# A fused attention and feed-forward backward kernel: dV up to eight heads ahead of dK, and the columns of dq as a stream of four a head

## The chip, the cores and the metric

The kernel runs on one core of a Trainium2 chip. The metric is device microseconds (us) of one execution. The kernel before takes 1714.82 us, the median of three runs (1712.49 to 1715.11); the execution whose profile is read below took 1712.58 us, and its trace spans 1710.6 us.

The profile calls the engines PE (TensorE; PEld are its weight loads), DVE (VectorE), ACT (ScalarE), POOL (GpSimd) and SP (SyncE). In this kernel SP computes nothing. It issues nearly all large DMAs, one after another in program order. An issue that has to wait for something holds up every issue behind it.

## What is computed

A decode step of a transformer block with one new token for each of 4 sequences, and its whole backward pass. Cut to what matters:

```python
# B=4 sequences, H=32 heads, Sk=4096 cached keys, Dh=128, D=512, F=1792, all bf16
q = layernorm(x) @ wq                                  # (4, 32, 1, 128)
p = softmax(einsum("bhqd,bhkd->bhqk", q, k_cache) * Dh ** -0.5)
o = einsum("bhqk,bhkd->bhqd", p, v_cache)
h = x + o @ wo
out = h + (silu(ln(h) @ w1) * (ln(h) @ w3)) @ w2
# outputs: out and the gradients of x, k_cache, v_cache, wq, wo, w1, w3, w2
```

There are 4 * 32 = 128 pairs of sequence and head, called heads here. Each has 1 MB of K and 1 MB of V. For one head, with the row dO of 128 numbers, P of 4096 numbers and the number c = sum(dO * O):

```python
dV = outer(P, dO)                  # 4096 x 128: needs P and dO, not V
dP = V @ dO                        # needs V read a second time, and transposed
dS = P * (dP - c) * scale
dK = outer(dS, q)                  # 4096 x 128
dq = scale * (M @ dO - c * kP)     # M is a 128x128 matrix, kept from the forward part
```

So the forward part reads K and V (256 MB), and the backward part reads V again (128 MB) and writes dV and dK (256 MB).

## The kernel before

SBUF is cut into 23 slots of 1 MB each. A tile of K, V, dK or dV takes a slot from a queue of free ones and gives it back. The next user of the slot waits, by semaphore, until the last one is done with it, and for a written gradient that means until its DMA has landed. During the forward part 8 slots fill up with the matrices M, 16 heads to a slot; they are free only when the columns of dq have been computed from them.

The functions of the backward part that the change and the prediction touch:

```python
def outer(dst, col2, row):                      # one DVE multiply of 128x4096
    nc.vector.tensor_tensor(out=..., in0=col2..., in1=row..., op=ALU.mult)

def grad_V(s):
    gv = Slot("gv")
    outer(gv.heads(), P2s.pop(s), reps["rdo", s // REP][:, s % REP, :])
    nc.sync.dma_start(out=rows_of(out_3[b, h]), in_=gv.heads())
    ...                                          # gives the slot back (0 and 1: later)

def front(s):                                    # dP of head s
    hl = s % B
    for g in range(SJ // GW):                    # 4 groups of 8 transposes on PE,
        V_T(s, psT, range(g, g + 1))             # each copied back by ACT
    ...
    dO_window(s + 2)                             # POOL
    ...  # 8 matmuls into rows["acc"]; after four heads one group of dP is complete
    # the slot of V goes to the ring of the V loads, or to the free ones

def group_dS(g): ...                             # DVE: dS of four heads at once

def grad_K(s):
    gk = Slot("gk")
    outer(gk.heads(), dS2s[s // B][:, s % B], reps["rq", s // REP][:, s % REP, :])
    nc.sync.dma_start(out=rows_of(out_2[b, h]), in_=gk.heads())
    gk.give()

def P_pairs(s): ...                              # POOL: P of a head in pairs, 3 buffers
def load_V2(eng): ...                            # SP: the second load of V
```

The side work is a generator that is advanced by some steps a head. It begins with the columns of dq:

```python
def side_work():
    ...
    for s in range(NH):
        nc.tensor.matmul(dq_ps[:, s:s + 1], lhsT=M_of(s)[:, 0:Dh], rhs=dOT_f[:, s:s + 1], start=True, stop=True)
        if s % MC == MC - 1:
            Ms[s // MC].give()
            ...                                  # loads wq again into a freed slot
        if s % 3 == 2:
            yield
    ...                                          # then dq, dx, and the gradients of the weights
```

A second generator, `rest_of_dO` (unit "o"), computes dO for the heads from 32 on; it runs from head 2, one step a head. The main loop:

```python
O0, S0, L, LV = 2, 21, 5, 3
for s in range(L):                               # lead-in
    load_ahead(s); P_pairs(s); front(s)
    if s < 2:
        first_gv[s].give()                       # slots of dV 0 and 1
    elif s < LV + 1:
        grad_V(s)                                # dV of heads 2 and 3
group_dS(0)
for s in range(NH):
    load_ahead(s + L)
    if s % REP == 0 and s + REP < NH:
        replicate(s + REP)                       # rows of dO and of q on all partitions
    P_pairs(s + L)
    if s + L < NH:
        front(s + L)
    ...
    if s > 0 and s + LV < NH:
        grad_V(s + LV)                           # dV three heads ahead
    grad_K(s)
    if s % B == B - 1 and s + 1 < NH:
        group_dS((s + 1) // B)
    if s >= S0:
        step("s", 3 if s < S0 + 15 else 2)
    elif s >= O0:
        step("o")
```

Of the kernel before, what the change touches and what calls it, by code (L numbers as in the profile page):

```python
# [9 lines left out]
FP32 = mybir.dt.float32  # L10
# [14 lines left out]
def kernel(  # L25
# [22 lines left out]
    nc = tc.nc  # L48
    P = nc.NUM_PARTITIONS
# [5 lines left out]
    Dh = A_k_cache.shape[3]  # L55
    F = B_w1.shape[1]
    NH = B * H
    HD = H * Dh
    assert NH == P and Dh == P and H == 32 and Sk == 32 * P
    assert D == 4 * P and F % P == 0  # L60
    DC = D // P
# [5 lines left out]
    MC = 16  # L67
# [3 lines left out]
    x2 = A_x.rearrange("b s d -> (b s) d")  # L71
# [12 lines left out]
    def bh_of(s):  # L84
        return s % B, s // B

    def rows_of(ap):
        return ap.rearrange("(p j) d -> p j d", p=P)
# [74 lines left out]
    ident_b = const.tile([P, P], BF16, name="ident_b")  # L163
# [14 lines left out]
    def ones_window(col):  # L178
# [11 lines left out]
                          in_=rowg[:, None, :, None].to_broadcast([P, 4, 8, 4]))  # L190
# [70 lines left out]
    with ExitStack() as c0:  # L261
# [11 lines left out]
        for h in range(H):  # L273
            for cc in range(DC):
                nc.tensor.matmul(qT_ps[:, h, :], lhsT=wq_s[cc].b(HD)[:, h * Dh:(h + 1) * Dh], rhs=xhatT[:, cc, :],
                                 start=(cc == 0), stop=(cc == DC - 1))
# [4 lines left out]
        for r in range(2):  # L281
            for t_ in range(2):
                for q in range(4):
                    nc.tensor.matmul(qr_ps[32 * q:32 * (q + 1), 2 * r + t_, :], lhsT=ident_b[:, 64 * r + t_:64 * (r + 1):2],
                                     rhs=qT_bf[:], start=True, stop=True, tile_position=(0, 32 * q))
# [3 lines left out]
    Ms = []  # L289

    def M_of(s):
        return Ms[s // MC].f(MC * (Dh + 1)).rearrange("p (n c) -> p n c", c=Dh + 1)[:, s % MC, :]
# [214 lines left out]
    def d_hh_units():  # L507
        w2 = load_w2()
        w2T = two_slots("w2T")
        gT = fw.tile([P, DC, B], BF16, name="gT", tag="gT", bufs=1)  # L510
        yield
        yield
        pt = psX.tile([P, DC, B], FP32, tag="x", name="pt_gT")
        for c in range(DC):
            nc.tensor.transpose(pt[:, c, :], gr[0:B, c * P:(c + 1) * P], ident_f[0:B, 0:B])
        nc.vector.tensor_copy(out=gT[:], in_=pt[:])
        nc.vector.tensor_copy(out=grT[:], in_=pt[:])
        gr_s.give()
        yield
        for jj in range(DC):  # L520
            for i in range(2):
                pt = psT.tile([P, GW, P], BF16, tag="tps", name="pt_w2")
                for k in range(7):
                    nc.tensor.transpose(pt[:, k, :], w2_view(w2, 7 * i + k)[:, jj * P:(jj + 1) * P], ident_b[:])
                nc.scalar.copy(out=w13_view(w2T, jj).rearrange("q (p c) -> q p c", c=FC)[:, :, i * 7:(i + 1) * 7],
                               in_=pt[:, 0:7, :].rearrange("q c p -> q p c"))
                yield
        for sl in w2:
            sl.give()
        ps = psX.tile([P, FC, B], FP32, tag="x", name="dhh_ps")  # L530
        for fc in range(FC):
            for jj in range(DC):
                nc.tensor.matmul(ps[:, fc, :], lhsT=w13_view(w2T, jj)[:, fc * P:(fc + 1) * P], rhs=gT[:, jj, :],
                                 start=(jj == 0), stop=(jj == DC - 1))
        nc.vector.tensor_copy(out=d_hhT[:], in_=ps[:])
        for sl in w2T:
            sl.give()
# [60 lines left out]
    units = {"d": d_hh_units()}  # L598

    def step(k, n=1):  # L600
        for _ in range(n):
            next(units[k], None)
# [113 lines left out]
    dOT_f = pers2.tile([P, NH], FP32, name="dOT_f")  # L716
    dOrows_bf = pers2.tile([NH, Dh], BF16, name="dOrows_bf")
# [4 lines left out]
    qrows_bf = pers2.tile([NH, Dh], BF16, name="qrows_bf")  # L722
# [29 lines left out]
    REP = B  # L752
    reps = {}
# [13 lines left out]
    P2s, first_gv = {}, []  # L767
# [9 lines left out]
    def grad_V(s):  # L777
        b, h = bh_of(s)
# [3 lines that stand above are left out]
        if s > 1:  # L782
            gv.give()
        else:
            first_gv.append(gv)
# [14 lines left out]
    with ExitStack() as cm:  # L800
# [33 lines left out]
        for wi, wt in enumerate((w1, w3)):  # L834
            for fc in range(FC):
                for cc in range(DC):
                    nc.tensor.matmul(gu_ps[:, wi, fc, :], lhsT=w13_view(wt, cc)[:, fc * P:(fc + 1) * P], rhs=hhatT[:, cc, :],
                                     start=(cc == 0), stop=(cc == DC - 1))
# [25 lines left out]
        for jj in range(DC):  # L864
            i_mm = 0
            for (lt, wt) in ((d_gateT_bf, w1), (d_upT_bf, w3)):
                for fc in range(FC):
                    nc.tensor.matmul(dn_ps[:, jj, :], lhsT=w13_view(wt, jj)[:, fc * P:(fc + 1) * P], rhs=lt[:, fc, :],
                                     start=(i_mm == 0), stop=(i_mm == 2 * FC - 1))
                    i_mm += 1  # L870
        for sl in w1 + w3:
            sl.give()
        rs = Slot("reps")
        rep_bufs = {nm_: [rs.b()[:, (2 * k + i) * 512:(2 * k + i + 1) * 512].rearrange("p (i d) -> p i d", i=REP) for i in range(2)]
                    for k, nm_ in enumerate(("rq", "rdo"))}
# [4 lines left out]
        ps = psA.tile([P, REP, Dh], FP32, tag="rT", name="repq_ps")  # L880
# [4 lines left out]
        for s in range(3):  # L885
# [8 lines left out]
                         start=True, stop=True)  # L894
# [14 lines left out]
        for b0, b1 in ((0, 1), (1, B)):  # L909
            ps = psA.tile([P, B, Dh], FP32, tag="rT", name="rep_ps")  # L910
            for b in range(b0, b1):
                for jj in range(DC):
                    nc.tensor.matmul(ps[:, b, :], lhsT=dhT[:, jj, b:b + 1].to_broadcast([P, P]), rhs=wo_page(0)[:, 0, jj, :],
                                     start=(jj == 0), stop=(jj == DC - 1))
# [12 lines left out]
    with ExitStack() as c2:  # L927
        psT = c2.enter_context(tc.tile_pool(name="psT2", bufs=2, space=bass.MemoryType.PSUM))
        psD = c2.enter_context(tc.tile_pool(name="psD", bufs=1, space=bass.MemoryType.PSUM))
        psrep = c2.enter_context(tc.tile_pool(name="psrep", bufs=1, space=bass.MemoryType.PSUM))  # L930
        psg = c2.enter_context(tc.tile_pool(name="psg", bufs=2, space=bass.MemoryType.PSUM))
        psx = c2.enter_context(tc.tile_pool(name="psx", bufs=1, space=bass.MemoryType.PSUM))
# [15 lines left out]
            gu.append((dst, ps, n))  # L948


        def side_work():
            pt = psg.tile([P, Dh], BF16, tag="gps", name="pt_O")
            nc.tensor.transpose(pt[:], OT_bf[:], ident_b[:])
            nc.scalar.copy(out=O_sb[:], in_=pt[:])
            dq_ps = psx.tile([P, 512], FP32, tag="x2", name="dq_ps")
            wq2s = deque()

            def load_wq2(cc):
                if cc < DC:
                    wq2s.append(Slot("wq2"))  # L960
                    nc.sync.dma_start(out=wq2s[-1].b(HD), in_=A_wq[cc * P:(cc + 1) * P, :])

            for s in range(NH):
                nc.tensor.matmul(dq_ps[:, s:s + 1], lhsT=M_of(s)[:, 0:Dh], rhs=dOT_f[:, s:s + 1], start=True, stop=True)
                if s % MC == MC - 1:
                    Ms[s // MC].give()
                    if s // MC in (3, 5):
                        load_wq2(s // MC // 2 - 1)
                if s % 3 == 2:
                    yield  # L970
            yield
            t = rs.f(2080)[:, 1536:1536 + NH]
            nc.vector.tensor_tensor(out=t, in0=c_rep[:], in1=kPT[:], op=ALU.mult)
# [13 lines left out]
            for cc in range(DC):  # L987
                wq2 = wq2s.popleft()
# [8 lines left out]
                for h in range(H):  # L997
                    nc.tensor.matmul(dx_ps[0:B, cc * P:(cc + 1) * P], lhsT=dqT_bf[:, h * B:(h + 1) * B], rhs=wv[:, h, :],
                                     start=(h == 0), stop=(h == H - 1))
# [62 lines left out]
            for i in range(2):  # L1062
                st = Slot("gw2")
                hw = hh_rows[:, i * 7 * P:(i + 1) * 7 * P].rearrange("b (p k) -> b k p", k=7)
                for k in range(7):
# [4 lines left out]
                                  in_=st.b(7 * D).rearrange("p (c j) -> p c j", c=7))  # L1070
# [4 lines left out]
            for (rows, out_ap) in ((dg_rows, out_6), (du_rows, out_7)):  # L1075
                for i in range(2):
                    st = Slot("gw13")
                    nw = hhat_bf[0:B, i * 2 * P:(i + 1) * 2 * P].rearrange("b (p k) -> b k p", k=2)
                    for k in range(2):
                        for (f0_, w_) in f_chunks:  # L1080
# [5 lines left out]
                                      in_=st.b(2 * F).rearrange("p (c f) -> p c f", c=2))  # L1086
                    st.give()
            r1.give()
            for h0 in range(0, H, 8):
                st = Slot("gwo")  # L1090
                ow = oflat.b(HD)[0:B, h0 * P:(h0 + 8) * P].rearrange("b (p k) -> b k p", k=8)
                for k in range(8):
# [4 lines left out]
                                  in_=st.b(8 * D).rearrange("p (k j) -> p k j", k=8))  # L1097
                st.give()
            oflat.give()
            r2.give()  # L1100

        units["s"] = side_work()


# [13 lines left out]
            nc.scalar.copy(out=dh, in_=dr_ps[:])  # L1118

        units["o"] = rest_of_dO()  # L1120
        def replicate(i0):
            K_ = 8 * B if i0 < 8 * B else P
            for nm_, rows in (("rdo", dOrows_bf), ("rq", qrows_bf)):
                if (nm_, i0 // REP) in reps:
                    continue
                ps = psrep.tile([P, REP, Dh], FP32, tag="rep", name="rep_ps")
                for i in range(REP):
                    nc.tensor.matmul(ps[:, i, :], lhsT=ident_b[0:K_, i0 + i:i0 + i + 1].to_broadcast([K_, P]), rhs=rows[0:K_, :],
                                     start=True, stop=True)
                rt = rep_bufs[nm_][i0 // REP % 2]  # L1130
                nc.scalar.copy(out=rt, in_=ps[:])  # L1131
                reps[nm_, i0 // REP] = rt

        rows = {}
        dS2s = {}
# [4 lines left out]
        def dO_window(s):  # L1140
            if s < NH:
                nc.gpsimd.tensor_copy(out=zd[s % B][:, 32:132:67], in_=dOT_bf[:, s:s + 1].to_broadcast([P, 2]))  # L1142

        def P_pairs(s):
            if s < NH and s not in P2s:
                P2s[s] = bw3.tile([P, SJ, 2], BF16, tag="P2", name="P2")
                nc.gpsimd.tensor_copy(out=P2s[s][:], in_=P_all[:, s, :, None].to_broadcast([P, SJ, 2]))  # L1147
# [58 lines left out]
                load_V2(nc.sync)  # L1206


        O0, S0, L, LV = 2, 21, 5, 3

        def load_ahead(s):
            prefetch()
# [2 lines left out]

        for s in range(2):
            dO_window(s)
        for s in range(L):
            load_ahead(s)
            P_pairs(s)  # L1220
            front(s)
            if s < 2:
                first_gv[s].give()
            elif s < LV + 1:
                grad_V(s)
        group_dS(0)
        for s in range(NH):
            load_ahead(s + L)
            if s % REP == 0 and s + REP < NH:
                replicate(s + REP)  # L1230
            P_pairs(s + L)
            if s + L < NH:
                front(s + L)
            elif s + L == NH:
                rows_out()
                rows_T()
            if s > 0 and s + LV < NH:
                grad_V(s + LV)
            grad_K(s)
            if s % B == B - 1 and s + 1 < NH:  # L1240
                group_dS((s + 1) // B)
            if s >= S0:
                step("s", 3 if s < S0 + 15 else 2)
            elif s >= O0:
                step("o")
        step("s", 400)


# [28 lines left out]
```

## Time and profile before

| what | value |
|---|---|
| median of three runs | 1714.82 us |
| span of the trace | 1710.6 us |
| moved by DMA | 707.50 MB: 422.59 MB of HBM read, 282.34 MB written |
| mean rate | 414 GB/s |
| busiest engines | PE 73%, DVE 72%, ACT 57%, POOL 24% |
| one outer product, dV or dK | 2.29 us of DVE, 128 of each |
| one head's four copies of transposed V | 4 x 1025 ns of ACT |
| DMA of one dV, issue to landing | 4.3 us at the least, 20.0 median |

The page of the profile gives the busy share of each engine, a row of rates in 40 slices of the span (42.8 us each), the chain of work that ended last, and groups of instructions. Finer views of the trace used below are tables of stretches of time, the timeline of an engine, and the list of waits. In a table of stretches each line gives, after the stretch, its length and the busy time of PE, PEld, DVE, ACT and POOL with the number of instructions; the last three numbers are the granted TensorE clock as a fraction, the DMA share and the GB/s.

### The profile page before, as it was taken

Reading aid. Unit: us, or ns where it says so; the run is one execution under the profiler, and the core shown is the slowest. Engines: PE = TensorE matmul, PEld = TensorE weight load, DVE = VectorE, ACT = ScalarE, POOL = GpSimd, SP = SyncE. Lnnn points to the kernel's source line nnn. Section 1 sums busy time; section 2 is a strip of 40 time slices with the busy share of each in tenths; the row PEclk is TensorE's granted clock in tenths of the full one; section 3 lists DMA queues with packets and bytes.
Section 4 is the critical chain, followed back from the end, with each engine's and each line's share of the span. In section 5 each row is a group of like instructions: output and inputs, shape, how many; then the busy total and the mean of one; then the engine's idle time right before and its main releaser. Section 6 shows DMA issues by size and latency. Waiting matters only on the chain. (4 is left out here: it accounts for less than half of the span.)

```text
span 1710.6 us, 38404 instructions
## 1 busy us (share of the span) xinstructions
PE 1253.6 (73%) x16180; PEld 928.1 (54%) x16180; DVE 1236.0 (72%) x1294; ACT 968.4 (57%) x1502; POOL 410.8 (24%) x680
## 2 busy tenths in 40 slices
PE   5889888888888888776689977766566665666650
PEld 4777766767676666644467755533344433443440
DVE  5989999999998996467677457765476566566672
ACT  3556444544544444677664468775668665675540
POOL 1211232222222321132112146420022223300220
PEclk9999999999999999899886589995889787787775
DMA  9999999999999999899999999999999999999996
GB/s 401 424 425 423 425 423 425 424 424 423 416 423 411 422 407 399 311 389 426 425 425 426 426 397 425 425 426 426 426 426 426 425 424 420 424 423 413 410 424 280
DMA packets 101741, 707.50 MB, mean 414 GB/s; under 512 B 11052, under 2 KB 15288, under 8 KB 17600
## 3 DMA queue, kind: packets, MB, share of 16 engines
q1 hardware_dynamic: 101152, 704.95, 99.0%
q8 instruction: 127, 2.08, 0.5%
q14 instruction: 46, 0.38, 0.1%
q0 software_dynamic: 416, 0.10, 0.0%
HBM read 422.59 MB, written 282.34 MB: 412 GB/s over the span
## 5 line engine op out<-in xcount | busy, mean ns | idle before, releaser
L765 ACT COPY V<-pt_tps 128x1024 bf16<-128x1024 bf16 x512 | 490.2, 1025 | 146.3 <-PE pt_tps L764 124.3
L764 PE MATMUL pt_tps<-ident_b,V 128*128 128x128 bf16 x4096 | 359.1, 249 | 206.3 <-ACT V L765 178.9
L764 PEld LDWEIGHTS <-V 128*128 128x128 bf16 x4096 | 306.7, 114 | 271.1 <-issue 231.1
L770 DVE TENSOR_TENSOR gv<-P,reps 128x4096 bf16<-128x4096 bf16 x125 | 286.9, 2295 | 162.9 <-DMA out_dram<-gv 115.5
L770 DVE TENSOR_TENSOR gk<-dS,reps 128x4096 bf16<-128x4096 bf16 x128 | 293.3, 2293 | 95.3 <-DMA out_dram<-gv 85.4
L421 DVE TENSOR_TENSOR PK<-Kn,PK 128x4096 bf16<-128x4096 bf16 x128 | 292.4, 2284 | 26.1 <-POOL PK L417 25.7
L436 PE MATMUL M_ps<-PK,Vn 128*128 128x130 bf16 x4096 | 285.2, 222 | 30.9 <-DMA Vn<-in_A_v_cache_dram 30.4
L436 PEld LDWEIGHTS <-Vn 128*128 128x128 bf16 x4096 | 253.2, 99 | 50.5 <-DMA Vn<-in_A_v_cache_dram 42.0
L1147 POOL COPY P<-P_all 128x64 bf16<-128x64 bf16 x127 | 121.5, 957 | 552.7 <-DVE gv L770 547.6
L328 DVE STREAM_TRANSPOSE KT<-Kn 128x512 f32<-128x512 f32 (+1 forms) x321 | 250.7, 797 | 0.3 <-issue 0.2
L323 ACT COPY KT<-pt_tps 128x1024 bf16<-128x1024 bf16 x128 | 129.5, 1012 | 184.9 <-PE pt_tps L322 150.1
L1177 PE MATMUL dP_ps<-V,zd 128*32 128x512 bf16 x1024 | 182.9, 439 | 66.7 <-ACT V L765 64.0
L334 POOL TENSOR_TENSOR W<-qrep,wmask 128x128 bf16<-128x128 bf16 x128 | 124.0, 969 | 82.1 <-PE S_ps L354 67.4
L417 POOL COPY PK<-P_all 128x64 bf16<-128x64 bf16 x128 | 32.6, 255 | 414.3 <-ACT P_all L411 411.3
L1142 POOL COPY zd<-dOT_bf 128x2 bf16<-128x2 bf16 x128 | 116.2, 908 | 65.7 <-PE dP_ps L1177 65.7
L1177 PEld LDWEIGHTS <-zd 128*32 128x32 bf16 x1024 | 37.6, 95 | 156.3 <-issue 141.1
L1131 ACT CAST reps<-rep_ps 128x512 bf16<-128x512 f32 x62 | 36.4, 586 | 129.4 <-DVE gk L770 97.7
L1191 DVE TENSOR_SCALAR dPr<-dPT_ps,c_rep 128x32 f32<-128x32 f32 x128 | 23.2, 242 | 89.3 <-PE dPT_ps L1159 89.2
L411 ACT COPY P_all<-pt_P 32x64 bf16<-32x64 bf16 x256 | 52.1, 204 | 53.2 <-PE pt_P L407 50.9
L322 PE MATMUL pt_tps<-ident_b,Kn 128*128 128x128 bf16 x1024 | 80.5, 223 | 0.0
L446 PE MATMUL kP_ps<-PK,onesw 128*32 128x512 bf16 x1024 | 79.2, 386 | 0.0
L386 ACT ACTIVATE E<-S_ps,nm 128x256 f32<-128x256 f32 x64 | 30.4, 475 | 82.0 <-DVE nm L383 82.0
(239 smaller groups left out, 1315.0 us busy)
## 6 DMA issues: line engine op xcount, KB each, us to landing
Kn<-in_A_k_cache_dram SPq DMA_DIRECT2D x128, 1024.0 KB, 15.3
Vn<-in_A_v_cache_dram SPq DMA_DIRECT2D x128, 1024.0 KB, 15.6
V<-in_A_v_cache_dram SPq DMA_DIRECT2D x128, 1024.0 KB, 19.8
out_dram<-gv SPq DMA_DIRECT2D x128, 1024.0 KB, 20.0
out_dram<-gk SPq DMA_DIRECT2D x128, 1024.0 KB, 20.1
wq<-in_A_wq_dram SPq DMA_DIRECT2D x8, 1024.0 KB, 15.5
out_dram<-gw SPq DMA_DIRECT2D x6, 896.0 KB, 19.7
wo<-in_A_wo_dram SPq DMA_DIRECT2D x4, 1024.0 KB, 11.7
```

The source lines that it names most:

```text
L322: nc.tensor.transpose(pt[:, i, :], Kn[:, c * GW + i, :], ident_b[:])
L323: nc.scalar.copy(out=KT[:, c * GW:(c + 1) * GW, :], in_=pt[:])
L328: nc.vector.transpose(out=KT[:, c * w_:(c + n) * w_], in_=Kn[:, c * w_:(c + n) * w_])
L334: nc.gpsimd.tensor_tensor(out=W[:, hl], in0=qrep[:, :, s:s + 1].to_broadcast([P, 4, 32]), in1=wmask[:, hl, None, :].to_broadcast([P, 4, 32 ...
L421: nc.vector.tensor_tensor(out=PK[:, :, 0:Dh].rearrange("p j (r t) -> p j r t", t=2), in0=Ks[s].heads().rearrange("p j (r t) -> p j r t", t=2),
L436: nc.tensor.matmul(hold["M"][:], lhsT=Vn[:, j, :], rhs=PK[:, j, :], start=(j == 0), stop=(j == SJ - 1))
L764: nc.tensor.transpose(pt[:, i, :], v[:, g * GW + i, :], ident_b[:])
L765: nc.scalar.copy(out=v[:, g * GW:(g + 1) * GW, :], in_=pt[:])
L770: nc.vector.tensor_tensor(out=dst.rearrange("p j (r t) -> p j r t", t=2), in0=col2[:, :, None, :].to_broadcast([P, SJ, Dh // 2, 2]), in1=r ...
L1142: nc.gpsimd.tensor_copy(out=zd[s % B][:, 32:132:67], in_=dOT_bf[:, s:s + 1].to_broadcast([P, 2]))
L1147: nc.gpsimd.tensor_copy(out=P2s[s][:], in_=P_all[:, s, :, None].to_broadcast([P, SJ, 2]))
L1177: nc.tensor.matmul(rows["acc"][32 * c:32 * (c + 1), :], lhsT=zq_window(zd[hl], 2 * hl + u), rhs=VT[:, j0:j0 + 4, :], start=(hl == 0 and u ...
```

## The change

It does four things in the backward part.

- In the lead-in, while the first V tiles are still being transposed, dV is computed up to head 8 and no longer only up to head 3; in the main loop dV stays up to eight heads ahead of dK. From head 60 on the lead shrinks, and from head 76 it is three again.
- The rows of dO and of q are replicated each at their own pace, dO's with dV and q's two heads before they are needed.
- The columns of dq become a stream of their own, four a head in heads 2 to 33, beside the work on dO. Before, they came nine a head in heads 21 to 35, three in each of three steps.
- The rest of the side work begins at head 35, two steps a head.

It is meant to give the DMA queues something to write while V is on its way through the transposes, and to free the slots of M earlier and without a stretch of dense PE work. No output is computed differently.

```diff
+        def dq_work():
+            for s in range(NH):
+                nc.tensor.matmul(dq_ps[:, s:s + 1], lhsT=M_of(s)[:, 0:Dh], rhs=dOT_f[:, s:s + 1], start=True, stop=True)
+                if s % MC == MC - 1:
+                    Ms[s // MC].give()
+                    if s // MC in (5, 6):
+                        load_wq2(s // MC - 5)
+                if s % 4 == 3:
+                    yield
+
+        units["q"] = dq_work()
...
         def side_work():
...
-            for s in range(NH):
-                nc.tensor.matmul(dq_ps[:, s:s + 1], lhsT=M_of(s)[:, 0:Dh], rhs=dOT_f[:, s:s + 1], start=True, stop=True)
...
-        def replicate(i0):
+        def replicate(nm_, i0):
...
-        O0, S0, L, LV = 2, 21, 5, 3
+        O0, S0, S1, L = 2, 21, 35, 5
+        gvd = {"n": 2}
+
+        def more_V(upto):
+            while gvd["n"] < min(NH, upto):
+                s = gvd["n"]
+                P_pairs(s)
+                replicate("rdo", s - s % REP)
+                grad_V(s)
+                P_pairs(s + 1)
+                P_pairs(s + 2)
+                gvd["n"] += 1
+                if s % REP == 2:
+                    replicate("rdo", s + 2)
+
+        def lead_V(s):
+            return 8 - min(5, max(0, s - 56) // 4)
...
+        for s in range(3, 6):
+            P_pairs(s)
         for s in range(L):
             load_ahead(s)
-            P_pairs(s)
             front(s)
-            if s < 2:
-                first_gv[s].give()
-            elif s < LV + 1:
-                grad_V(s)
+            if s == 0:
+                for gv in first_gv:
+                    gv.give()
+            more_V((4, 6, 7, 8, 9)[s])
+            if s == 0:
+                replicate("rdo", REP)
         group_dS(0)
         for s in range(NH):
             load_ahead(s + L)
-            if s % REP == 0 and s + REP < NH:
-                replicate(s + REP)
-            P_pairs(s + L)
+            if s % REP == 2:
+                replicate("rq", s + 2)
...
-            if s > 0 and s + LV < NH:
-                grad_V(s + LV)
+            if s > 0:
+                more_V(s + 1 + lead_V(s))
             grad_K(s)
...
-            if s >= S0:
-                step("s", 3 if s < S0 + 15 else 2)
+            if O0 <= s < S0:
+                step("o")
+            if s >= S1:
+                step("s", 2)
             elif s >= O0:
-                step("o")
+                step("q")
```

More of the change, by code (lines that the diff above doesn't have):

```diff
@@ L948, in grad_unit, with load_wq2 @@
             gu.append((dst, ps, n))
+        wq2s = deque()
+        def load_wq2(cc):
+            if cc < DC:
+                wq2s.append(Slot("wq2"))
+                nc.sync.dma_start(out=wq2s[-1].b(HD), in_=A_wq[cc * P:(cc + 1) * P, :])
+        dq_ps = psx.tile([P, 512], FP32, tag="x2", name="dq_ps")
+        def dq_work():
[8 more added lines that the diff above has]
+        units["q"] = dq_work()
         def side_work():
@@ L954, in side_work @@
             nc.scalar.copy(out=O_sb[:], in_=pt[:])
[L955 to L961, printed above, removed]
-            for s in range(NH):
-                nc.tensor.matmul(dq_ps[:, s:s + 1], lhsT=M_of(s)[:, 0:Dh], rhs=dOT_f[:, s:s + 1], start=True, stop=True)
[L965 to L970, printed above, removed]
             yield
@@ L1120 @@
         units["o"] = rest_of_dO()
-        def replicate(i0):
+        def replicate(nm_, i0):
+            if i0 >= NH or (nm_, i0 // REP) in reps:
+                return
             K_ = 8 * B if i0 < 8 * B else P
[L1123 to L1132, printed above, removed]
+            rows = dOrows_bf if nm_ == "rdo" else qrows_bf
+            ps = psrep.tile([P, REP, Dh], FP32, tag="rep", name="rep_ps")
+            for i in range(REP):
+                nc.tensor.matmul(ps[:, i, :], lhsT=ident_b[0:K_, i0 + i:i0 + i + 1].to_broadcast([K_, P]), rhs=rows[0:K_, :],
+                                 start=True, stop=True)
+            rt = rep_bufs[nm_][i0 // REP % 2]
+            nc.scalar.copy(out=rt, in_=ps[:])
+            reps[nm_, i0 // REP] = rt
         rows = {}
```

## The prediction

> **What bounds the kernel now.** I read the page first: the engines' shares, the row of slices and the queues.
>
> ```profile
> PE 1253.6 (73%) x16180; PEld 928.1 (54%) x16180; DVE 1236.0 (72%) x1294; ACT 968.4 (57%) x1502; POOL 410.8 (24%) x680
> ...
> GB/s 401 424 425 423 425 423 425 424 424 423 416 423 411 422 407 399 311 389 426 425 425 426 426 397 425 425 426 426 426 426 426 425 424 420 424 423 413 410 424 280
> ...
> q1 hardware_dynamic: 101152, 704.95, 99.0%
> ```
>
> No compute engine is above 73%, but the rate sits at 424 to 426 GB/s in most slices. 707.50 MB at 425 GB/s are 1664.7 us; the span is 1710.6. So 46 us at most are lost anywhere to DMA that is not at its rate, and a change that moves the same bytes can win only from these. The lowest slices are 16 to 18 (311 in the middle), slice 24 (397) and the last. A table of stretches of 20 us placed the slices 16 to 18 between the two parts of the kernel, and stretches of 4 us show the hole:
>
> ```profile
> 708.00:712.00 4.00, 3.01 (x31) 1.65 (x29) 1.54 (x1) 2.72 (x4) 0.36 (x2) 0.83 0.64 262
> 712.00:716.00 4.00, 3.11 (x37) 1.90 (x37) 0.00 (x0) 2.77 (x4) 0.36 (x2) 1.00 0.00 0
> 716.00:720.00 4.00, 2.50 (x31) 1.47 (x28) 0.00 (x0) 3.73 (x4) 0.00 (x0) 1.00 0.85 211
> 720.00:724.00 4.00, 3.05 (x41) 2.30 (x36) 0.69 (x4) 2.99 (x4) 0.36 (x2) 1.00 0.96 373
> 724.00:728.00 4.00, 2.79 (x32) 1.57 (x31) 3.82 (x4) 2.53 (x5) 0.91 (x1) 1.00 0.73 244
> 728.00:732.00 4.00, 2.50 (x29) 1.37 (x26) 4.00 (x3) 3.62 (x4) 2.24 (x1) 1.00 0.94 305
> 732.00:736.00 4.00, 3.04 (x40) 2.06 (x36) 2.26 (x2) 3.14 (x4) 1.63 (x2) 1.00 1.04 313
> 736.00:740.00 4.00, 2.50 (x34) 1.71 (x33) 1.70 (x1) 2.77 (x4) 0.43 (x1) 1.00 0.93 363
> ```
>
> The reader should look at the last column and, in the same lines, at the third busy time, DVE: it does nothing from 712 to 720. Against 424 GB/s these eight lines miss 162 + 424 + 213 + 51 + 180 + 119 + 111 + 61 = 1321 GB/s over 4 us each, 5.28 MB, which is 12.5 us. From 740 us on the rate is 424 again. The timeline of DVE says why it is idle:
>
> ```profile
> 704.83 2.29 DVE L770 TENSOR_TENSOR gv<-reps 128x4096 bf16<-128x4096 bf16 x1 [2.01 <-PE dP_ps L1177]
> 707.25 2.29 DVE L770 TENSOR_TENSOR gv<-P,reps 128x4096 bf16<-128x4096 bf16 x1
> 723.31 0.73 DVE L1191 TENSOR_SCALAR dPr<-dPT_ps,c_rep 128x32 f32<-128x32 f32 x4 [13.77 <-PE dPT_ps L1159]
> ```
>
> After dV of heads 2 and 3 the program has nothing for DVE until the dP of four heads is complete. Those come at 5.0 us a head, in a loop of PE transposes and ACT copies (3.76 us of copies and a gap of 1.23 us). And SP makes the hole worse:
>
> ```profile
> 700.22 7.26 SPq L781 DMA_DIRECT2D out_dram<-gv  x3
> 715.45 0.34 SPq L797 DMA_DIRECT2D V<-in_A_v_cache_dram  x1
> 715.88 0.38 SPq L781 DMA_DIRECT2D out_dram<-gv  x1
> ```
>
> The fourth dV is ready at 709.5 but goes out at 715.88, because a V load stands before it in SP's order, waiting for the slot of head 2.
>
> Slice 24 comes from the dq columns, which lie from 871 to 998 us by the tile's first and last start:
>
> ```profile
> 744.00:871.00 127.00, 87.29 (x1009) 57.83 (x1008) 87.99 (x71) 90.66 (x106) 28.11 (x39) 0.92 1.01 425
> 871.00:998.00 127.00, 113.19 (x862) 90.97 (x857) 71.61 (x51) 59.70 (x67) 22.69 (x28) 0.64 1.01 421
> 998.00:1040.00 42.00, 31.38 (x376) 22.54 (x376) 36.49 (x23) 32.45 (x38) 30.06 (x21) 0.92 1.01 410
> ```
>
> PE is 89% busy there at a clock of 0.64, and 128 / 9 = 14.2 heads take 127 us, 8.9 us a head. Three transfers of 1.049 MB at 424 GB/s are 7.42 us a head. The stretch lives off writes and loads queued before it, and when they are used up the rate falls: 395 and 394 GB/s in the stretches 980 to 1000 and 1000 to 1020, a loss of (29 + 30) * 20 / 424 = 2.8 us.
>
> **What the Trainium skill says.** "DMA: Bandwidth & Descriptors", section "Where 436 GB/s comes from", names 435 GB/s as the ceiling of the 16 ports into SBUF and reports 425 for long transfers. The trace agrees: 424 to 426 in full stretches. So I treat 424 as a ceiling that no order of work raises. "Perfetto Trace Analysis", section "Identifying the Most-Contended Engine", says to judge DMA by bandwidth and not by occupancy. This trace shows why: from 732 to 736 the DMA share is 1.04 at 313 GB/s. "TensorE: Matmul & The Clock Gate", section "What's actually happening", gives two clocks, half and full, set by recent activity in windows of 3413 ns. The dq stretch agrees, most of its stretches of 5 us lying at 0.50 to 0.84. The dq matmuls have a single column, so I count a burst of them as time in which PE may fall to half clock.
>
> **The change, part by part.** Bytes, DVE, POOL and PE instructions are the same in number, apart from order; so only the times at which DMA has work matter.
>
> *The lead.* After dV 3 (709.5 us) DVE goes on with dV 4 to 8, five outer products of 2.29 us. They go through the free slots: three in rotation (those of dV 1, 2 and 3), a fourth once head 1 is done. A slot comes round after 2.29 us of DVE and at least 4.3 us to landing, 6.7 us with some handover; over three slots that is 2.2 us a product, so DVE is hardly held. dV 4 is then done at about 711.8, 5 at 714.1, 6 at 716.4, 7 at 718.7, 8 at 721, before dP of four heads is complete at 723.3. In SP's new order dV 0 to 6 all stand before the V load that blocked at 715.45, so none waits behind it; that load itself goes out about 1 us later. From about 710 the supply is one write per 2.3 us (456 GB/s) plus a V load every 5 us, more than 424. By 724 SP has issued six dV and two V loads since 709, 8.4 MB, of which 424 GB/s carry 6.4 MB in 15 us; the 2 MB left last 5 us, and from there dK 0, the next V load and dV 9 follow as before. So the hole should close from about 711 to 740. The eight lines miss 5.28 MB and the lead gives 5 * 1.049 = 5.24 MB: both bounds are 12.4 us. I take off 1.2 us, because the first DMA after 708 is not earlier than before and there may be short gaps around the V loads near 726 and 732. **Gain 11.2 us.** As the rest is bound by DMA, it passes on to the end.
>
> *The stream of dq.* Nine columns took 2.2 to 2.6 us on PE; four are about 1.1 us. A head in the loop takes 5.0 us at full clock, 0.9 with a unit of wo, 0.4 for its share of the replicated rows: 6.3, and 7.4 with dq. That is just the 7.42 us of DMA. At half clock the loop itself is 8.9 - 2.4 - 0.4 = 6.1 us in place of 5.0, so heads 2 to 20 may take up to 8.5 us, and heads 21 to 34, without wo, 6.5 to 7.6. On average over heads 2 to 34 it is the same PE work as before in the same time. The dense stretch and its 2.8 us of loss should go, but a thinner one may appear near 850 us. I count half of the 2.8 as gained (**1.4 us**) and put **1.5 us** against it for such dips.
>
> *Replication at its own pace* removes waits of ACT for the previous dK (97.7 us in the list of waits, 18 times). ACT is 57% busy and the rate is full in those stretches: 0.
>
> *Slots.* M's slots become free from head 5 on, not 22. That deepens the queue of writes while DMA is already full: 0. From head 35 the side work stands within one step of where it stood, and from head 76 the lead is 3 again, so the end, 1660 to 1710.6, stays: 0.
>
> Sum: -11.2 - 1.4 + 1.5 = -11.1 us; 1714.8 - 11.1 = 1703.7, rounded to 1703.5.
>
> **Rivals.**
> 1. *DVE and the slots hold the lead back.* If the writes of dV land in 8 us and more, the three slots give one product in 3.4 us or slower, and half the hole stays: about 1709. For it: in the list of waits of 690 to 760 us DVE waited 10.1 us for dV's DMA. Against: those waits are at 737 and later, with the queue refilling.
> 2. *dq between heads 2 and 20 makes PE the bound.* 19 heads by 1 us over the DMA's pace are 19 us, less a stock of 4 to 6 MB in the queues (10 to 14 us): 5 to 9 us lost, which leaves about 1709 to 1713. For it: the clock of 0.64 with dq. Against: bursts of 1.1 us and not 2.4, and PE at 69% from 744 to 871.
> 3. *The hole is hidden anyway*, the data being caught up later by something else: 1714. Against: the rate afterwards is at its ceiling, so nothing can catch up.
> 4. *Everything works*: 12.4 + 2.8 us, 1699.6.
>
> **Range and chances.** The low end is just below rival 4, 1699; the high end, 1711, holds rival 1 and most of rival 2. Faster by 2% would be 1680.5, more than all the losses after 690 us other than the end: 1 in 100. Slower by 2% (1749) would need PE-bound stretches of 45 us in sum: 2 in 100.
>
> **What would show it.** Right: in the stretches from 712 to 740 the rate is above 400 and DVE computes five dV products before the first dS; nothing below 410 GB/s around 990 and 1010; the last slices as before; the mean rate near 417 GB/s. Wrong: stretches below 400 between 760 and 1000 with PE above 85% busy and a low clock (rival 2), or DVE waiting for dV's DMA between 709 and 722 (rival 1). If the hole closes and the time does not fall by at least 8 us, then a later stretch has to run below its former rate, and the table of stretches will say which.

## The result and the profile after

The kernel after takes 1702.36 us, the median of four runs (1701.74 to 1702.93); the kernel before, beside it, 1714.96 (1712.49 to 1715.16). The ratio is 0.993, with a 95% interval of 0.9913 to 0.9947: 12.6 us less. In a later series the same kernel took 1703.63 us beside 1714.09 (ratio 0.9938, 0.9925 to 0.995), 10.5 us less. The prediction said 1703.5.

The page of the kernel after, its busy times and its row of rates:

```profile
PE 1242.4 (73%) x16180; PEld 915.5 (54%) x16180; DVE 1236.5 (73%) x1294; ACT 968.9 (57%) x1502; POOL 406.4 (24%) x678
...
GB/s 401 424 424 424 424 424 424 424 423 424 417 422 412 423 405 400 385 415 425 425 424 426 425 426 426 425 426 426 425 423 420 419 423 417 423 420 414 416 423 275
```

The engines are as busy as they were, and the bytes on the main queue are the same, 704.95 MB. The slice that had 311 GB/s has 385, the one with 397 has 426, and the last ones are as low as they were. The 4 us stretches of the kernel after show what became of the hole; the last number is GB/s, the one before it the DMA share, the third busy time is DVE:

```profile
708.00:712.00 4.00, 3.47 (x33) 2.35 (x33) 4.00 (x2) 2.75 (x3) 1.92 (x1) 0.74 0.88 363
712.00:716.00 4.00, 2.47 (x30) 1.56 (x28) 3.54 (x3) 3.76 (x4) 2.98 (x5) 1.00 1.01 418
716.00:720.00 4.00, 3.02 (x41) 2.19 (x40) 4.00 (x3) 3.03 (x4) 2.72 (x2) 1.00 1.01 420
720.00:724.00 4.00, 2.76 (x33) 1.62 (x32) 1.66 (x1) 2.72 (x5) 2.07 (x3) 1.00 1.03 270
724.00:728.00 4.00, 3.20 (x36) 1.88 (x33) 3.05 (x6) 2.81 (x4) 0.41 (x1) 1.00 0.95 383
728.00:732.00 4.00, 2.50 (x32) 1.54 (x29) 4.00 (x3) 3.76 (x4) 2.69 (x2) 1.00 1.01 422
732.00:736.00 4.00, 3.04 (x40) 2.04 (x36) 1.40 (x2) 2.96 (x4) 0.47 (x2) 1.00 1.01 428
736.00:740.00 4.00, 2.81 (x34) 1.78 (x34) 1.72 (x1) 3.00 (x4) 0.44 (x2) 1.00 1.01 426
```

These lines miss 61 + 6 + 4 + 154 + 41 + 2 - 4 - 2 = 262 GB/s against 424, where before it was 1321: (1321 - 262) * 4 / 424 = 10.0 us of DMA time won. Only 720 to 728 is still a dip. The DVE timeline of the kernel after:

```profile
707.74 6.72 DVE L770 TENSOR_TENSOR gv<-P,reps 128x4096 bf16<-128x4096 bf16 x3
714.92 6.73 DVE L770 TENSOR_TENSOR gv<-P,reps 128x4096 bf16<-128x4096 bf16 x3 [0.46 <-POOL P L1152]
724.88 0.72 DVE L1196 TENSOR_SCALAR dPr<-dPT_ps,c_rep 128x32 f32<-128x32 f32 x4 [3.22 <-PE dPT_ps L1164]
```

Six dV follow one another with one pause of 0.46 us, none of them waiting for a slot, and the wait for the first dS has shrunk from 13.77 us to 3.22. In SP's timeline seven dV stand in one entry, and the V load comes after them:

```profile
700.91 16.66 SPq L781 DMA_DIRECT2D out_dram<-gv  x7
717.68 0.76 SPq L797 DMA_DIRECT2D V<-in_A_v_cache_dram  x1
```

The stretches in which dq lay before, in the kernel after:

```profile
744.00:871.00 127.00, 102.96 (x1142) 77.77 (x1142) 92.71 (x73) 90.13 (x103) 47.10 (x39) 0.91 1.01 425
871.00:998.00 127.00, 89.61 (x967) 62.78 (x966) 85.15 (x59) 82.81 (x97) 34.99 (x42) 0.95 1.01 425
998.00:1040.00 42.00, 23.07 (x276) 15.80 (x275) 23.92 (x21) 23.77 (x27) 5.14 (x12) 0.89 1.01 426
```

PE is now 81% and 71% busy in the first two, in place of 69% and 89%, at a clock of 0.91 and 0.95, and the rate is 425 throughout.

To follow the losses from kernel to kernel I use one measure: (425 - rate) / 425 * length, from the rate of a long stretch. The rates are whole GB/s, so one unit is 0.2 us in a stretch of 80 us. For 700 to 780 us it gives 13.9 us before (351 GB/s) and 3.6 after (406), for 960 to 1040 us 2.8 before (410) and -0.2 after (426). The two together are 13.3 us.

### The profile page after: what moved, and what is told of

It reads as the page before. It is cut to its first block, busy times and chain, and to the rows that moved or that the text cites. A ratio compares the mean times of both kernels' runs of the same rounds, so it can differ in the third digit from the quotient of the medians.

```text
span 1700.1 us, 38407 instructions
## 1 busy us (share of the span) xinstructions
PE 1242.4 (73%) x16180; PEld 915.5 (54%) x16180; DVE 1236.5 (73%) x1294; ACT 968.9 (57%) x1502; POOL 406.4 (24%) x678
## 3 DMA queue, kind: packets, MB, share of 16 engines
q1 hardware_dynamic: 101152, 704.95, 99.4%
## 4 chain that ended last, share of the span: by engine, by line
DMA 37%; ACT 10%; PE 7%; issue 1%; DVE 1%; DVEq 0%; SPq 0%; ACTq 0%; POOL 0%
DMA out_dram<-gv 14%; DMA out_dram<-gk 12%; DMA V<-in_A_v_cache_dram 9%; ACT V L765 9%; PE pt_tps L764 2%; PE dq_ps L962 2%; PE dP_ps L1182 2%; DMA out_dram<-gwo 1%; DVE gk L770 1%; DVE gv L770 1%; PE rep_ps L1133 0%; ACT dPr L1157 0%; PE pt_wo L574 0%; ACT reps L1136 0%; PE o_ps L1059 0%
## 5 line engine op out<-in xcount | busy, mean ns | idle before, releaser
L764 PE MATMUL pt_tps<-ident_b,V 128*128 128x128 bf16 x4096 | 353.3, 247 | 192.4 <-ACT V L765 152.9
L764 PEld LDWEIGHTS <-V 128*128 128x128 bf16 x4096 | 303.1, 113 | 264.0 <-issue 199.0
L1152 POOL COPY P<-P_all 128x64 bf16<-128x64 bf16 x125 | 100.5, 806 | 447.3 <-DVE gv L770 440.0
L1147 POOL COPY zd<-dOT_bf 128x2 bf16<-128x2 bf16 x128 | 131.4, 1028 | 155.3 <-PE dP_ps L1182 155.2
L322 PEld LDWEIGHTS <-Kn 128*128 128x128 bf16 x1024 | 62.0, 100 | 25.8 <-issue 25.8
L354 PE MATMUL S_ps<-KT,W 128*32 128x256 bf16 x1536 | 75.3, 285 | 0.5 <-DVE KT L328 0.2
```

Of the source, the lines that this page charges most:

```text
L322: nc.tensor.transpose(pt[:, i, :], Kn[:, c * GW + i, :], ident_b[:])
L764: nc.tensor.transpose(pt[:, i, :], v[:, g * GW + i, :], ident_b[:])
```

## The experiments

Two parts of the change may have closed the two holes: the lead of dV and the stream of dq. Every run stood beside the kernel before on the same chip, and the differences below are from the median of those. The runs of the kernel before alone spread over 3 to 5 us in a series, so a difference of 1 or 2 us between two medians says little.

| kernel | median us | beside before | ratio (95%) | short of 425 at 700 to 780 | at 960 to 1040 |
|---|---|---|---|---|---|
| lead alone | 1702.58 | 1713.96 | 0.9933 (0.9921 to 0.9946) | 3.6 us | 0.0 us |
| dq stream alone | 1713.13 | 1713.96 | 0.9994 (0.9986 to 1.0002) | 13.9 | 0.0 |
| before, loads behind the fronts | 1709.02 | 1713.96 | 0.9977 (0.9967 to 0.9988) | 8.8 | 0.6 |
| lead given back at once | 1703.66 | 1713.96 | 0.9939 (0.9926 to 0.9953) | 7.0 | -0.2 |
| lead of six | 1706.67 | 1714.09 | 0.9957 (0.9945 to 0.997) | 6.8 | 0.0 |
| lead of nine | 1703.31 | 1714.09 | 0.9937 (0.9923 to 0.995) | 4.0 | -0.2 |
| before, SP order swapped | 1714.30 | 1714.09 | 1.0001 (0.9993 to 1.0009) | 13.7 | 4.3 |
| after, once more | 1703.63 | 1714.09 | 0.9938 (0.9925 to 0.995) | 4.1 | 0.0 |
| lead of eight and two more V | 1708.78 | 1714.48 | 0.9967 (0.9958 to 0.9977) | 8.7 | 0.0 |
| lead of ten | 1703.39 | 1714.48 | 0.994 (0.9926 to 0.9954) | 4.0 | 0.0 |

### The lead alone

```diff
 def dq_work():
-                if s % 4 == 3:
+                if s % 3 == 2:
                     yield
...
-            if s >= S1:
-                step("s", 2)
-            elif s >= O0:
-                step("q")
+            if s >= S0:
+                step("q", 3)
+            if s >= S1:
+                step("s", 2)
```

The second load of wq also goes back to the places it had before.

> The kernel after, but the columns of dq again nine a head in heads 21 to 35. Theory (the gain is the two holes of the DMA rate added up, 10.0 us at 708 to 740 and 2.8 us at 980 to 1020): the first hole stays closed, the second comes back with a rate near 395 GB/s, PE above 85% busy and a clock near 0.64 in the dq stretch; about 1705, 2 to 3 us above the kernel after. Rival (the dq stream gives nothing, the dip near 1000 is a chance of the run or belongs to something else): about 1702 to 1703, no dip or the same as after. Second rival (the deeper stock of dV that the lead leaves in the queues carries the dense stretch too): no dip, 1702.

1702.58 us, 11.4 less than before, the whole gain. The dense stretch is back, as the stretches of this kernel show:

```profile
871.00:998.00 127.00, 114.31 (x867) 91.44 (x867) 78.25 (x56) 63.55 (x73) 30.98 (x35) 0.63 1.01 426
998.00:1040.00 42.00, 29.19 (x383) 20.87 (x379) 31.16 (x19) 33.78 (x39) 22.76 (x15) 1.00 1.01 425
```

PE is 90% busy at a clock of 0.63, as before (89%, 0.64), and still no rate is lost. The first theory falls at this point and its second rival holds. What differs is the stock of transfers that have been issued and have not landed. It can be read from the time that a V load takes from issue to landing, the last number of the DMA issues, here for 960 to 1000 us in the kernel before:

```profile
V<-in_A_v_cache_dram SPq DMA_DIRECT2D x5, 1024.0 KB, 13.7
```

and for the same stretch with the lead alone:

```profile
V<-in_A_v_cache_dram SPq DMA_DIRECT2D x6, 1024.0 KB, 20.0
```

At 425 GB/s, 20.0 us are 8.1 transfers of 1.049 MB in flight and 13.7 us are 5.6. Counted from the times of issue and landing in the traces, never more than eight transfers of SP are in flight in either kernel; what sets this limit is not shown. From 871 to 940 us both have 8.0 on average, so 20 us says only that the eight places are full, not how much is ready behind them. Before, they then ran down, to 5.5 on average from 980 to 1000 us. With the lead alone they were still 7.9 there, and the dense stretch ended at 991.7 us.

A rival is left here, for this kernel also has the new pace of replication and the later side work. The kernel before with two more V loads, an experiment further down, has neither, and its stretch is as dense:

```profile
871.00:998.00 127.00, 111.79 (x858) 89.60 (x856) 74.67 (x55) 62.60 (x71) 28.65 (x33) 0.65 1.01 426
```

It is 0.6 us short at 960 to 1040 us, where the kernel before is 2.8 and its version with SP's order swapped 4.3. So transfers made early carry the stretch without the other parts of the change.

### The dq stream alone

```diff
-            if s == 0:
-                for gv in first_gv:
-                    gv.give()
-            more_V((4, 6, 7, 8, 9)[s])
+            if s < 2:
+                first_gv[s].give()
+            more_V((2, 2, 3, 4, 4)[s])
...
-            return 8 - min(5, max(0, s - 56) // 4)
+            return 3
```

> The kernel after, but dV three heads ahead of dK throughout, as before; the dq stream and the new pace of the replications stay. Theory: the hole at 708 to 740 is as in the kernel before (12 us short of 424 GB/s), the dip near 1000 is gone: about 1712, 2.8 us below before. Rival (dq beside the work on dO makes PE the bound in heads 2 to 20): stretches below 400 GB/s between 760 and 900 and a time of 1715 or more. Second rival (most of the gain comes from slots of M that are free earlier): 1708 or less.

1713.13 us; the interval of the ratio holds 1. The stretches of this kernel:

```profile
712.00:716.00 4.00, 2.46 (x31) 1.58 (x30) 0.00 (x0) 2.72 (x4) 0.19 (x1) 1.00 0.26 102
...
744.00:871.00 127.00, 102.33 (x1153) 76.85 (x1150) 91.84 (x72) 89.73 (x103) 38.08 (x39) 0.92 1.01 425
871.00:998.00 127.00, 89.51 (x974) 62.48 (x974) 86.66 (x60) 84.29 (x99) 38.86 (x43) 0.96 1.01 425
```

The first hole is as deep as before (13.9 us at 700 to 780) and the dip near 1000 us is gone. dq beside the work on dO does not make PE the bound: 425 GB/s at a PE of 81%. So the stream does remove the second hole by itself, but the 2.8 us that this should bring are not seen in the time (0.8 us, not told from zero). In this trace other stretches were slower than in that of the kernel before: 1240 to 1640 us ran at 419 GB/s in place of 421, 1.8 us. And slots of M that become free earlier bring nothing that can be measured.

### The place of dV 3 in SP's order

The prediction blamed SP for part of the hole. The first attempt to test that did something else:

```diff
 for s in range(L):
-            load_ahead(s)
             P_pairs(s)
             front(s)
             if s < 2:
                 first_gv[s].give()
             elif s < LV + 1:
                 grad_V(s)
+            load_ahead(s)
```

> The kernel before, with one change: in the lead-in the load of the next V stands behind the write of dV in SP's order, so that dV 3 goes out when it is ready (near 709.6 us) and not behind the V load at 715.9. Theory (the hole is a lack of results; a write that is only early leaves the same lack a few us later): the same bytes have gone out by 724 us, 1714 to 1715. Rival (SP's order makes the hole, as the prediction said in part): the empty 4 us at 712 to 716 are filled and stay filled, 2.5 us gained, about 1712.5.

1709.02 us, 4.9 less than before: more than either expected. But the order of dV 3 and the tenth V had not changed. `load_ahead` loads a V if its head has none; behind the front, which uses V up, that is always so, and it loaded two more V from free slots. SP's timeline of this run shows the pair, the tenth and the eleventh V, at 704.90, where the kernel before has the tenth at 715.45; dV 3 comes at 717.70:

```profile
700.86 2.87 SPq L781 DMA_DIRECT2D out_dram<-gv  x2
704.90 2.24 SPq L797 DMA_DIRECT2D V<-in_A_v_cache_dram  x2
...
717.70 0.34 SPq L781 DMA_DIRECT2D out_dram<-gv  x1
```

Two transfers of 1.049 MB at 425 GB/s are 4.9 us, and the trace is 5.1 us less short at 700 to 780 us (8.8 and 13.9), although DVE made dV 2 at 710.33 us only, not at 704.83, after 6.87 us without work. So the run says something of the hole after all: it can be filled with reads as well as with writes. That the time agrees to the tenth is chance, for the interval of the ratio means 2.1 to 5.7 us. The test that was meant is this, on the kernel before:

```diff
 for s in range(L):
-            load_ahead(s)
+            if s != LV:
+                load_ahead(s)
             ...
             elif s < LV + 1:
                 grad_V(s)
+            if s == LV:
+                prefetch()
```

> The kernel before with SP's order swapped at one place: the write of dV 3 stands before the load of the tenth V and goes out near 709.6 us, not at 715.9. No load is added. Theory (the hole is a lack of transfers, their order does not matter): the 4 us without any transfer at 712 to 716 are filled and 716 to 724 are emptier by the same, time as before within 1 us, 1713 to 1715. Rival (the place of dV 3 in SP's order was part of the cause): 2 us or more below before, 1712 or less.

1714.30 us, ratio 1.0001. The order is as wanted, the fourth dV goes out before the load:

```profile
700.86 9.25 SPq L781 DMA_DIRECT2D out_dram<-gv  x4
715.24 5.33 SPq L797 DMA_DIRECT2D V<-in_A_v_cache_dram  x2
```

and the hole has only moved to the right: the five stretches from 708 to 728 us had 262, 0, 211, 373, 244 GB/s in the kernel before and have 410, 127, 262, 217, 88 here, two of them shown:

```profile
712.00:716.00 4.00, 3.15 (x40) 1.95 (x38) 0.00 (x0) 2.77 (x4) 0.36 (x2) 1.00 0.30 127
...
724.00:728.00 4.00, 2.79 (x32) 1.62 (x30) 3.86 (x3) 2.53 (x5) 0.91 (x1) 1.00 0.32 88
```

The wait in SP's order cost nothing here, because the transfer that it held up found the DMA engines empty a few us later as well.

### How long a lead

```diff
-            more_V((4, 6, 7, 8, 9)[s])
+            more_V((4, 5, 6, 7, 7)[s])         # six; (4, 6, 7, 8, 10) for nine, (4, 6, 7, 9, 11) for ten
...
-            return 8 - min(5, max(0, s - 56) // 4)
+            return 6 - min(3, max(0, s - 56) // 4)   # 9 - min(6, ..) for nine, 10 - min(7, ..) for ten
```

> The kernel after with a lead of six heads in place of eight (dV up to head 6 in the lead-in). Theory (each dV written in the hole takes one transfer, 1.049 MB at 425 GB/s or 2.47 us, off the time, until the hole is full): three more dV than before are 7.4 us in place of the 10.3 measured with five, so about 1705, and some 6.5 us short of 425 GB/s from 700 to 780 us. Rival (what counts is only that DVE and the queues never fall empty; three are enough for that): 1702 to 1703.

> The kernel after with a lead of nine heads: dV 9 is made at the end of the lead-in, where DVE has nothing to do for 3.2 us before the first dS and the rate is 270 and 383 GB/s from 720 to 728. Theory: that dip is a lack of results and is filled, 1.8 us gained, about 1700.5. Rival (the dip is one of the DMA itself, its share being 1.03 at 270 GB/s, and more work does not fill it): 1702 to 1703.

> The kernel after with a lead of ten heads (dV up to head 10 in the lead-in, one of them earlier than with nine). Theory (the hole is used up at eight; what is left is not a lack of results): 1702 to 1704, the dip at 720 to 728 as with nine, and the first dK waits behind dV on DVE. Rival (the lead goes on paying 2.5 us a head): 1698 to 1700.

The kernel after, unchanged, ran in the series of six and nine as their measure:

> The kernel after once more, unchanged, as a measure on the same chip for leads of six and nine: 1702 to 1703.

Six: 1706.67 us, 7.4 less than before, as three transfers of 2.47 us would give. The interval is 5.1 to 9.4 us; the trace at 700 to 780 us says 7.1 (6.8 short in place of 13.9). Eight, five transfers, gave 10.5 in the same series and 12.6 in the first, around the bound of 12.4. Nine (1703.31, 10.8 less) and ten (1703.39, 11.1 less) give no more than eight. With nine, DVE is busy for the ninth dV in the dip that is left, and the dip stays, as this kernel's stretches show:

```profile
720.00:724.00 4.00, 3.06 (x36) 1.85 (x36) 4.00 (x3) 2.78 (x4) 4.00 (x3) 1.00 1.02 332
724.00:728.00 4.00, 2.86 (x31) 1.84 (x29) 2.94 (x7) 3.94 (x5) 1.78 (x3) 1.00 0.90 328
```

The DMA share is 1.02 at 332 GB/s, and by issue and landing four or five transfers are in flight from 723.5 to 728 us. They take longer; they are not missing. The ninth dV itself is issued at 725.4 us and could help with the second half of the dip only. With ten, DVE meets the other limit and waits 3.08 us for a slot before dK 0:

```profile
731.12 2.29 DVE L770 TENSOR_TENSOR gk<-dS,reps 128x4096 bf16<-128x4096 bf16 x1 [3.08 <-DMA out_dram<-gv]
```

### The lead given back at once

```diff
 def lead_V(s):
-            return 8 - min(5, max(0, s - 56) // 4)
+            return 3
```

> The kernel after, but with the lead given back at once: dV up to head 8 in the lead-in as after, then none until dK has come within three heads, and three heads ahead from there. Theory (the lead is a stock of bytes written early; it pays only as long as DMA finds enough without it): in heads 1 to 5 a head brings only a V load and a dK, 2.1 MB per 6 us or so, 350 GB/s, and 5 to 7 us of the 10 are lost again: about 1707 to 1709, with rates below 400 between 725 and 765. Rival (only the early filling counts, holding the lead is needless): 1702 to 1703 with 424 GB/s from 728 on.

1703.66 us, 10.3 less than before (the kernel after: 12.6 and 10.5). The expected second hole is there, but later and smaller than thought:

```profile
756.00:760.00 4.00, 3.04 (x44) 2.69 (x43) 0.76 (x1) 3.59 (x4) 0.98 (x2) 1.00 0.97 299
760.00:764.00 4.00, 3.46 (x39) 2.36 (x39) 0.00 (x0) 2.61 (x4) 0.36 (x2) 1.00 1.02 348
764.00:768.00 4.00, 2.45 (x33) 1.54 (x31) 0.00 (x0) 3.92 (x5) 0.00 (x0) 1.00 0.90 248
```

In heads 1 to 5 the V loads and dK, with what the lead left in flight, keep DMA full until 756 us (426 GB/s from 752 to 756): by SP's timeline the V loads of 727.19, 732.18 and 737.17 are 5.0 us apart, and 2.1 MB in 5.0 us are 420 GB/s. Then (125 + 76 + 176) * 4 / 424 = 3.6 us are lost. In the time they cannot be told from the spread of the runs. So filling the hole is nearly all of the gain; that holding the lead afterwards brings anything is seen in the trace alone (7.0 us short at 700 to 780, where the kernel after has 3.6 and 4.1).

### Eight heads and two more V

```diff
 for s in range(L):
-            load_ahead(s)
             front(s)
             ...
             more_V((4, 6, 7, 8, 9)[s])
             if s == 0:
                 replicate("rdo", REP)
+            load_ahead(s)
```

> The kernel after, with the load of the next V behind the front of each head in the lead-in; as the earlier run with that edit showed, this also makes two more V loads, from free slots, so two slots fewer turn over for dV. In the first 16 us of the lead-in reads and writes are then mixed, where the kernel after writes seven dV in a row. Theory (the rest of the hole, some 2 us at 720 to 728, comes from a lack of transfers that more dV could not fill because their slots had not come back): a read needs no such slot, the dip shrinks, 1 to 2 us below the kernel after, about 1701. Rival (the dip belongs to DMA itself when V loads join a stream of writes): it stays or moves, 1702 to 1704. Second rival (two slots fewer hold DVE back): 1705 and more.

1708.78 us (1703.94 to 1711.2), 5.7 less than before, where the kernel after gave 12.6 and 10.5: the second rival holds. In the kernel after no dV of the lead-in waits for a slot; here three waits, of 1.95, 1.02 and 4.78 us, fall between 710 and 723 us. The longest, in the DVE timeline of this run:

```profile
722.52 6.73 DVE L770 TENSOR_TENSOR gv<-P,reps 128x4096 bf16<-128x4096 bf16 x3 [4.78 <-DMA out_dram<-gv]
```

Reads alone filled the hole by 4.9 us and writes alone by 10 to 12, but the two draw on the same slots and do not add up. No version tried beats the kernel after by more than the spread.

## Why the prediction was right, and where it was not

**What bounds the kernel.** Right. The bytes are the same in all variants, and the time follows what is lost against 424 to 426 GB/s, to within 1 to 3 us. Bytes moved into the hole paid about 2.47 us for each transfer of 1.049 MB (three dV 7.4 us, two V 4.9 us, with the intervals given above).

**The lead, predicted 11.2 us.** Right in mechanism and nearly in size: 10.0 us in the eight stretches, 10.3 in the long one (9.8 when run again), and 11.4 us in the time with the lead alone. The slots turned over as reckoned, and the last of the six dV ended at 721.65 us, where 721 was said. Rival 1 did not happen. The deduction of 1.2 us for gaps was too small: the dip at 720 to 728 alone costs (154 + 41) * 4 / 424 = 1.8 us. The prediction took it for granted that with 2 MB left over DMA would run at its rate there; it had four transfers in flight and did not.

**SP.** "And SP makes the hole worse" was wrong. Without that wait the time is the same within 0.1%. It was a wait that the trace shows truly, read as a cost without asking what the freed time would be filled with. It carried no term in the sum, so it did no harm to the number.

**The stream of dq, +1.4 us, and -1.5 us against it.** The step that failed is "the dense stretch and its 2.8 us of loss should go" as a gain of the stream. The loss went, and 2.8 us of it, not half. But the lead alone removes it too, with PE just as dense and as slow, because its stock outlasts the stretch (7.9 transfers in flight from 980 to 1000 us, 5.5 before). The stream alone also removes it, and its time shows nothing that can be told from zero. Beside the lead the stream is worth nothing measurable: 1702.58 without it, 1702.36 to 1703.63 with it. The deduction for thin dips near 850 us (rival 2) did not come about: 425 GB/s from 744 to 1040. In the sum the two terms cancel, so the 11.1 us is in effect the lead alone, and that the total fits says nothing for them. It is in part luck that it fits so closely: by the traces the change won 10.3 us at 700 to 780 and 3.0 at 960 to 1040, and lost 1.8 at 1240 to 1640 and 0.5 at the end, 11.0 in all.

**Replication and slots, 0 each.** Not seen apart, but both are in the dq stream alone, which gave 0.8 us or nothing. **The end, 0.** From 1640 us on 14.5 us are lost before and 15.0 after. Between 1240 and 1640 us, 3.8 before (421 GB/s) and 5.6 after (419); this was not foreseen and its cause stays open. It is in most variants with and without the lead, so it is not the lead's price.

## What to carry to other kernels

Where transfers bound a kernel and their rate is at its ceiling, look for the stretches in which it is not, and count what they miss in bytes. A change is worth the bytes it moves into such a hole, up to the hole's size and the free buffers, and a wait whose removal moves no bytes into it is worth nothing. A stretch that is too dense for one engine need not be thinned out if enough transfers are ready ahead of it. The time from issue to landing tells when they run out; while the queue is full, it does not tell how many more there are.

## What was not expected of the hardware

At 720 to 728 us the rate is 270 and 383 GB/s with a DMA share of 1.03 and 0.95, and every variant with a lead of eight to ten and no added V loads has a dip there (332 and 328 with nine). It begins 2 to 3 us after the issue of the first V load behind a run of seven writes (717.68 and 720 us in the kernel after). A lack of transfers is not the reason: in the kernel after two or three writes in flight gave 418 GB/s from 712 to 716 us, while the same four transfers, two V loads and two dV, were in flight from 723.3 to 727.5 us, and the rate went from 262 to 442 GB/s in that time. Such stretches are not peculiar to the lead: the kernel before has 313 GB/s at a share of 1.04 from 732 to 736 us, and the lead given back has 348 at 1.02 from 760 to 764 us, both with V loads and writes mixed. More dV do not fill the dip, and mixing reads in earlier could not be told apart from the lack of slots that it brought. Why the transfers take longer there stays open.
